# Linear attention and a gated feed-forward block: fewer dummies and another VectorE order in the first batch's start

## The chip, the cores and the metric

The kernel runs on one core of a Trainium2 chip. The metric is the device time of one execution in microseconds (us), the median over runs. Times inside a profile are us from the start of its span, which is about 1.8 us shorter than the execution.

## The reference, cut to what matters

```
phi(x) = where(x > 0, x, exp(x) - 1) + 1            # = max(x, 0) + min(exp(x), 1)
kv  = einsum('bhsd,bhse->bhde', phi(k), v)
z   = sum_s phi(k)
num = einsum('bhsd,bhde->bhse', phi(q), kv)
den = einsum('bhsd,bhd->bhs', phi(q), z) + 1e-6
x   = (num / den), heads side by side               # 4608 x 512
out = (silu(x @ w_gate) * (x @ w_val)) @ w_out      # 512 -> 1536 -> 512
```

There are 8 batches of 8 heads, 576 tokens and 64 dimensions each. Everything after the first x is a long stream of matmuls; before it TensorE has little to do, because batch 0 must come from memory, be put through phi, and be summed into kv and z.

## The kernel before

The program fixes the order of each engine's instructions. Only the start of batch 0 is touched. The helpers, with the lines by which the profile names them:

```python
WARM = (4, 3, 4, 4, 2, 1, 2, 2)

def warm(n, ...):            # L124: n dummies, 128x512 matmuls of ones that nobody reads
def q_turn(lp, pair_):       # L430: 16 matmuls that turn half lp of q into PSUM
    for l2 in range(2):
        for j in range(J - 1):
            nc.tensor.matmul(out=pair_[j // 4][...], lhsT=qr[0][:, 2 * lp + l2, ...], rhs=id16[:, :], ...)
def q_exp(lp, h, pair_):     # L120, ScalarE:  exp of a bank of turned q
def q_phi(lp, h, pair_):     # L442, VectorE:  max and min in one, completes phi(q)
def mx_k / mn_k / add_k:     # L143, L147, L159, VectorE: max(k, 0), min(exp(k), 1), their sum
def zt(...):                 # L396: z of half a batch, 9 matmuls for the max part, 9 for the min part
def zr_copy(...):            # L400, VectorE: z, spread to 64 columns
```

```python
    warm(WARM[0]); q_one(qa); q_one(qb)
    q_turn(0, qa);  q_exp(0, 0, qa);  q_exp(0, 1, qa)
    warm(WARM[1])
    q_turn(1, qb);  q_exp(1, 0, qb);  q_exp(1, 1, qb)
    warm(WARM[2])
    exp_k(0, 0);  exp_k(0, 1)
    q_phi(0, 0, qa);  q_phi(0, 1, qa)
    mx_k(0, 0)
    q_phi(1, 0, qb)
    mn_k(0, 0)
    mx_k(0, 1)
    zt(0, 0, X[1], kp, True, False)
    warm(WARM[3])
    zt(0, 0, X[1], ek, False, True)
    zr_copy(0, 0, X[1])
    warm(WARM[4])
    t_corners(0, Zr, 0, pp4[2]);  lnrd(pp4[2], 0)      # L254, then four log / exp on ScalarE
    mn_k(0, 1)
    q_phi(1, 1, qb)
    zt(0, 1, Y[0], kp, True, False)
    warm(WARM[5])
    zt(0, 1, Y[0], ek, False, True)
    add_k(0, 0)
    zr_copy(0, 1, Y[0])
    warm(WARM[6])
    kv_corner(0, 0, kp, True, True)                    # L185, the kv product
    ...                                                # then x, layer 1 (L276, from fb = 2 on L292)
```

q comes in two loads. Two of its four heads are cast to 16 bits first (one of them on ScalarE); the third and fourth head are cast on VectorE when the second load has landed.

Of the kernel before, what the change touches and what calls it, by code (L numbers as in the profile page):

```python
# [17 lines left out]
def kernel(  # L18
# [21 lines left out]
    EPS = 1e-6  # L40
    SC = 4096.0
    NB = 3
    WARM = (4, 3, 4, 4, 2, 1, 2, 2)

    sb = ctx.enter_context(tc.tile_pool(name="sb", bufs=1))
    pp = ctx.enter_context(tc.tile_pool(name="ps", bufs=1, space=bass.MemoryType.PSUM))
# [72 lines left out]
    def act(out, in_, func=AF.Copy, scale=1.0, bias=0.0):  # L119
        nc.scalar.activation(out=out, in_=in_, func=func, bias=bias, scale=scale)  # L120

    def warm(n, w=512, ps=None):
        for _ in range(n):
            nc.tensor.matmul(out=(ps or pp4[1][1])[:, 512 - w:512], lhsT=ones[:, :],  # L124
                             rhs=ones[:, 0:1].to_broadcast([P, w]), start=True, stop=True)
# [4 lines left out]
    def jl(t, b, lp):  # L130
        return t[b % 2][:, lp, :, :].rearrange("p j (l d) -> p l j d", d=D)

    def lj(t, b, lp):
        return t[b % NB][:, hs(lp), :].rearrange("p l (j d) -> p l j d", d=D)

    def exp_k(b, lp):
        act(jl(ek, b, lp), lj(kr, b, lp), AF.Exp)
# [4 lines left out]
    def mx_k(b, lp):  # L142
        nc.vector.tensor_scalar(out=jl(kp, b, lp), in0=lj(kr, b, lp), scalar1=0.0, scalar2=None, op0=ALU.max)  # L143

    def mn_k(b, lp):
        a = ek[b % 2][:, lp, :, :]
        nc.vector.tensor_scalar(out=a, in0=a, scalar1=1.0, scalar2=None, op0=ALU.min)  # L147
# [246 lines left out]
    def zt(b, lp, ps, t, first, last):  # L394
        for j in range(J):
            nc.tensor.matmul(out=ps[:, 0:2], lhsT=t[b % 2][:, lp, j, :], rhs=ob[:, 0:P:C],  # L396
                             start=(first and j == 0), stop=(last and j == J - 1))

    def zr_copy(b, lp, ps):
        nc.vector.tensor_scalar(out=Zr[b][:, lp, :, :], in0=ps[:, 0:2].unsqueeze(2).to_broadcast([P, 2, D]),  # L400
                                scalar1=1.0 / SC, scalar2=None, op0=ALU.mult)

    def lnrd(ps, i, w0=0, w1=512, early=False):
        for l2 in range(2):
            act(lnt[2 * i + l2][:, w0:w1], ps[l2][:, w0:w1], AF.Ln, bias=epsb[:, 0:1])
            if not early:
                act(rd[i][:, l2, w0:w1], lnt[2 * i + l2][:, w0:w1], AF.Exp, scale=-1.0)
        for l2 in range(2 if early else 0):
            act(rd[i][:, l2, w0:w1], lnt[2 * i + l2][:, w0:w1], AF.Exp, scale=-1.0)
# [8 lines left out]
    def t_corners(g, W, lp, ps):  # L418
        for (b, j0, j1, c0) in units(g)[1]:
            corners(ps, W[b], b, lp, j0, j1, c0)  # L420

    def q_one(pair_):
        for h in range(2):
            nc.tensor.matmul(out=pair_[h][:, :], lhsT=part[:, :], rhs=ones[:, 0:1].to_broadcast([P, 512]),
                             start=True, stop=False)

    def q_turn(lp, pair_):
        for l2 in range(2):
            for j in range(J - 1):
                nc.tensor.matmul(out=pair_[j // 4][D * l2:D * l2 + D, P * (j % 4):P * (j % 4) + P],  # L430
                                 lhsT=qr[0][:, 2 * lp + l2, D * j:D * j + D], rhs=id16[:, :],
                                 start=False, stop=(j % 4 == 3))

    def q_half(lp, h):
        return qT[0][:, lp, 4 * h:4 * h + 4, :, :].rearrange("p j h c -> p (j h c)")

    def q_exp(lp, h, pair_):
        act(q_half(lp, h), pair_[h][:, :], AF.Exp, bias=m1[:, 0:1])

    def q_phi(lp, h, pair_):  # L440
        a = q_half(lp, h)
        nc.vector.scalar_tensor_tensor(out=a, in0=pair_[h][:, :], scalar=1.0, in1=a, op0=ALU.max, op1=ALU.min)  # L442
# [4 lines left out]
    qa, qb = pp4[2], pp4[0]  # L447
# [3 lines left out]
    nc.vector.tensor_copy(out=qr[0][:, 3, :], in_=q32[:, 3, :])  # L451
    warm(WARM[0])
    q_one(qa)
# [3 lines left out]
    q_exp(0, 1, qa)  # L457
    warm(WARM[1])
    q_turn(1, qb)
    q_exp(1, 0, qb)  # L460
    q_exp(1, 1, qb)
    warm(WARM[2])
    exp_k(0, 0)
# [2 lines left out]
    q_phi(0, 1, qa)  # L466
    mx_k(0, 0)
    q_phi(1, 0, qb)
    mn_k(0, 0)
    mx_k(0, 1)  # L470
    zt(0, 0, X[1], kp, True, False)
    warm(WARM[3])
    zt(0, 0, X[1], ek, False, True)
    zr_copy(0, 0, X[1])
    warm(WARM[4])
    t_corners(0, Zr, 0, pp4[2])
    lnrd(pp4[2], 0)
    mn_k(0, 1)
    q_phi(1, 1, qb)
    zt(0, 1, Y[0], kp, True, False)  # L480
    warm(WARM[5])
    zt(0, 1, Y[0], ek, False, True)
# [279 lines left out]
```

## Time and profile before

| | |
|---|---|
| median of three runs | 315.97 us (315.6 to 316.2) |
| span of the profiled execution | 314.1 us |
| TensorE busy | 98% of the span |
| kv product of batch 0 starts | 13.07 |
| steady part of layer 1 starts (first L292) | 19.48 |

Two numbers serve as mile posts from here on: the start of the kv product (L185), and the start of layer 1's steady part (L292). How the page and the chain are read is told in the prediction.

### The profile page before, as it was taken

What the parts mean: (1) busy time and instruction counts of PE and PEld (TensorE: products, weight loads), DVE (VectorE), ACT (ScalarE), POOL (GpSimd) and SP (SyncE); (2) the same over time, 40 slices, a digit from 0 to 9 for tenths busy, and PEclk for the clock granted to TensorE, in tenths of its full rate; (3) what the DMA queues carried; (4) which work ended last, traced back from release to release, by engine and by line L of the source; (5) the groups of instructions that cost most, each with busy time, mean ns of one, the idle gap of its engine ahead of it and who ended that gap; (6) DMA issues with size and microseconds to landing.
All of it is one profiled execution on the core that took longest, in us unless ns stands there. A gap on an engine that the chain in (4) does not pass through costs nothing.

```text
span 314.1 us, 5531 instructions
## 1 busy us (share of the span) xinstructions
PE 307.5 (98%) x2186; PEld 142.7 (45%) x2186; DVE 205.5 (65%) x362; ACT 152.0 (48%) x231; POOL 48.0 (15%) x72
## 2 busy tenths in 40 slices
PE   8899999999999999999999999999999999999994
PEld 4444444444544454445444544444444444444442
DVE  4854688899789767977597849874991434133410
ACT  4865839738643745366535743475330333133311
POOL 7755334300000230023000500000000000000000
PEclk9999999999999999999999999999999999999999
DMA  8999999995612396129702990314032400140014
GB/s 216 198 198 199 206 207 232 238 206 88 140 33 41 50 180 170 38 41 163 197 20 57 134 230 0 75 35 102 0 61 59 91 1 1 37 98 0 2 33 100
DMA packets 41162, 32.80 MB, mean 104 GB/s; under 512 B 16432, under 2 KB 36144, under 8 KB 41136
## 3 DMA queue, kind: packets, MB, share of 16 engines
q0 software_dynamic: 20464, 18.29, 37.2%
q1 hardware_dynamic: 20592, 14.13, 18.6%
q8 instruction: 17, 0.28, 0.4%
q14 instruction: 9, 0.07, 0.1%
q10 hardware_dynamic: 80, 0.03, 0.0%
HBM read 37.75 MB, written 9.44 MB: 150 GB/s over the span
## 4 chain that ended last, share of the span: by engine, by line
PE 96%; DMA 1%; DVE 1%; ACT 1%; issue 0%
PE pp L292 57%; PE pp L299 30%; PE pp L276 2%; PE pp L254 2%; PE pp L185 2%; DMA q<-in_q_dram 1%; PE pp L124 1%; PE pp L430 1%; ACT qT L120 0%; ACT ek L120 0%; PE pp L371 0%; PE pp L396 0%; DVE kp L159 0%; PE pp L212 0%; DVE ek L147 0%; DVE osb L322 0%
## 5 line engine op out<-in xcount | busy, mean ns | idle before, releaser
L120 ACT ACTIVATE sil<-pp 128x512 f16<-128x512 f32 x108 | 63.4, 597 | 101.8 <-PE pp L292 100.9
L292 PE MATMUL pp<-xT,wg 128*128 128x512 f16 x416 | 106.8, 379 | 0.0
L292 PE MATMUL pp<-xT,wv 128*128 128x512 f16 x416 | 106.8, 379 | 0.0
L285 DVE SCALAR_TENSOR_TENSOR hT<-pp,sil 128x512 f16<-128x512 f32 x108 | 72.4, 682 | 49.0 <-PE pp L292 35.6
L299 PE MATMUL pp<-wo,hT 128*128 128x512 f16 (+2 forms) x444 | 97.2, 374 | 0.6 <-DVE osb L322 0.6
L299 PEld LDWEIGHTS <-hT 128*128 128x128 f16 x444 | 41.9, 98 | 49.7 <-issue 2.1
L292 PEld LDWEIGHTS <-wv 128*128 128x128 f16 x416 | 40.7, 98 | 49.1
L292 PEld LDWEIGHTS <-wg 128*128 128x128 f16 x416 | 40.7, 98 | 48.4
L322 DVE TENSOR_SCALAR osb<-pp 128x512 f32<-128x512 f32 (+1 forms) x19 | 12.9, 682 | 30.6 <-PE pp L299 26.2
L120 ACT ACTIVATE osb<-pp 128x512 f32<-128x512 f32 (+1 forms) x18 | 10.3, 573 | 34.8 <-PE pp L299 34.8
L120 ACT ACTIVATE ek<-kr 128x1152 f16<-128x1152 f16 x16 | 17.8, 1156 | 0.1
L120 ACT ACT_TABLE_LOAD x13 | 16.7, 1283 | 2.3 <-PE pp L292 2.1
L693 POOL COPY gate<-qT 128x1 f16<-128x1 f16 x4 | 1.3, 320 | 97.9 <-DVE hT L285 71.2
L229 DVE TENSOR_TENSOR qp<-qp,rden 128x1152 f16<-128x1152 f16 x12 | 16.2, 1347 | 0.0
L220 DVE TENSOR_REDUCE den<-prod 128x18 f32<-128x1152 f16 x12 | 16.1, 1344 | 0.0
L271 DVE TENSOR_SCALAR xT<-pp 128x512 f16<-128x512 f32 (+1 forms) x14 | 8.8, 667 | 7.1 <-PE pp L254 7.1
L120 ACT ACTIVATE eq<-qr 128x1152 f16<-128x1152 f16 x12 | 13.2, 1147 | 0.0
L103 POOL DMA_DIRECT2D vr<-in_v_dram x16 | 11.7, 735 | 9.3 <-PE pp L292 3.5
L103 POOL DMA_DIRECT2D kr<-in_k_dram x16 | 11.7, 735 | 7.8 <-DMA wo<-in_moe_w_out_dram 1.8
L147 DVE TENSOR_SCALAR ek<-ek 128x1152 f16<-128x1152 f16 x16 | 7.7, 483 | 7.5 <-ACT ek L120 7.5
L159 DVE TENSOR_TENSOR kp<-ek,kp 128x1152 f16<-128x1152 f16 x16 | 12.1, 758 | 0.5
L103 POOL DMA_DIRECT2D qr<-in_q_dram x14 | 10.1, 723 | 5.8 <-DMA wo<-in_moe_w_out_dram 1.8
(76 smaller groups left out, 183.6 us busy)
## 6 DMA issues: line engine op xcount, KB each, us to landing
out_dram<-osb SPq DMA_DIRECT2D x70, 128.0 KB, 3.2
kr<-in_k_dram POOLq DMA_DIRECT2D x16, 288.0 KB, 8.9
vr<-in_v_dram POOLq DMA_DIRECT2D x16, 288.0 KB, 9.8
qr<-in_q_dram POOLq DMA_DIRECT2D x14, 288.0 KB, 12.1
wo<-in_moe_w_out_dram POOLq DMA_DIRECT2D x3, 512.0 KB, 12.7
wg<-in_moe_w_gate_dram POOLq DMA_DIRECT2D x5, 256.0 KB, 9.1
wv<-in_moe_w_val_dram POOLq DMA_DIRECT2D x5, 256.0 KB, 9.7
q<-in_q_dram SPq DMA_DIRECT2D x2, 576.0 KB, 4.1
```

The source lines that it names most:

```text
L103: nc.gpsimd.dma_start(out=dst[b % NB][:, 2 * lp:2 * lp + 2, :], in_=src[b].rearrange("(l a) (c j) d -> (a c) l (j d)", a=2, j=J)[:, 2 * lp ...
L120: nc.scalar.activation(out=out, in_=in_, func=func, bias=bias, scale=scale)
L147: nc.vector.tensor_scalar(out=a, in0=a, scalar1=1.0, scalar2=None, op0=ALU.min)
L159: nc.vector.tensor_tensor(out=a, in0=ek[b % 2][:, lp, :, :], in1=a, op=ALU.add)
L185: nc.tensor.matmul(out=ps[hh][D * l2:D * l2 + D, D * lp:D * lp + D], lhsT=t[b % 2][rows, lp, j, D * l2:D * l2 + D], rhs=vr[b % NB][rows, 2 ...
L220: nc.vector.tensor_reduce(out=den[:, c, :], in_=prod[:, :, :].rearrange("p j (l d) -> p (j l) d", d=D), axis=AX.X, op=ALU.add)
L229: nc.vector.tensor_tensor(out=qv, in0=qv, in1=rden[:, c, :].unsqueeze(2).to_broadcast([P, 2 * J, D]), op=ALU.mult)
L271: nc.vector.tensor_scalar(out=dst, in0=ps[l2][:, c0:], scalar1=1.0 / SC, scalar2=None, op0=ALU.mult)
L285: nc.vector.scalar_tensor_tensor(out=hT[g % 2][:, fb, :], in0=ps[1][:, :], scalar=SC, in1=s[:, :], op0=ALU.mult, op1=ALU.mult)
L292: nc.tensor.matmul(out=ps[h][:, :], lhsT=w[:, c, P * fb:P * fb + P], rhs=xT[g % 2][:, c, :], start=(c == 0), stop=(c == 3))
L299: nc.tensor.matmul(out=l2p[(g, t)][:, n0:n1], lhsT=hT[g % 2][:, fb, P * t:P * t + P], rhs=wo[:, fb, n0:n1], start=(fb == 0), stop=(fb == F ...
L322: nc.vector.tensor_scalar(out=o[:, n0:n1], in0=ps[:, n0:n1], scalar1=1.0 / SC, scalar2=None, op0=ALU.mult)
```

## The change

The intent is to shorten the chain that leads to the first real work of TensorE. Two of three dummies between the turns of q's halves go. On VectorE q's last phi moves ahead of k's first min, into a wait, so that it no longer stands in front of the add of k, and the second half's max and min move behind the first z. One dummy more covers the longer wait ahead of z's second part.

```diff
-    WARM = (4, 3, 4, 4, 2, 1, 2, 2)
+    WARM = (4, 1, 4, 5, 2, 1, 2, 2)
...
     q_phi(1, 0, qb)
+    q_phi(1, 1, qb)
     mn_k(0, 0)
-    mx_k(0, 1)
     zt(0, 0, X[1], kp, True, False)
...
     lnrd(pp4[2], 0)
+    mx_k(0, 1)
     mn_k(0, 1)
-    q_phi(1, 1, qb)
     zt(0, 1, Y[0], kp, True, False)
```

## The prediction

> **What bounds the kernel now.** I read the page first (engines, then its chain), then the chain of waits in order of time for the first 45 us, then the timelines of TensorE (PE), VectorE (DVE) and ScalarE (ACT) for the first 34 us. Times are us from the start of the span.
>
> The page, parts 1 and 4:
>
> ```profile
> PE 307.5 (98%) x2186; PEld 142.7 (45%) x2186; DVE 205.5 (65%) x362; ACT 152.0 (48%) x231; POOL 48.0 (15%) x72
> PE 96%; DMA 1%; DVE 1%; ACT 1%; issue 0%
> ```
>
> TensorE carries nearly the whole span, so only what lets it reach its real work sooner is worth anything. The change touches the first 13 us alone. There the chain hops between engines (columns: start, length, what):
>
> ```profile
> 6.23 0.76 PE pp L124 x3
> 6.99 0.61 PE pp L430 x12
> 7.60 0.02 issue
> 7.62 1.26 ACT qT L120 x2
> 8.88 1.06 ACT ek L120
> 9.95 0.02 issue
> 9.97 0.66 DVE ek L147
> 10.62 0.05 issue
> 10.67 0.39 PE pp L396 x9
> ```
>
> L124 are the dummies (matmuls whose result nobody reads), L430 the turns of q's second half, then come q's two exponentials, k's first exponential, k's min and the second part of z. So three dummies sit on the path that sets the end. From about 19.6 on the chain is layer 1, matmul behind matmul, 80 in 17.27 us (0.216 each): whatever the start gains moves all of this earlier, unless weights are late.
>
> The VectorE timeline (start, length, then line, operation and tiles, in brackets the idle time before):
>
> ```profile
> 7.93 0.46 DVE L143 TENSOR_SCALAR kp<-kr 128x1152 f16<-128x1152 f16 x1
> 8.34 0.69 DVE L442 SCALAR_TENSOR_TENSOR qT<-pp,qT 128x512 f16<-128x512 f32 x1
> 9.97 0.64 DVE L147 TENSOR_SCALAR ek<-ek 128x1152 f16<-128x1152 f16 x1 [0.94 <-ACT ek L120]
> 10.54 0.44 DVE L143 TENSOR_SCALAR kp<-kr 128x1152 f16<-128x1152 f16 x1
> 11.10 0.29 DVE L400 TENSOR_SCALAR Zr<-pp 128x128 f16<-128x128 f32 x1
> 11.30 0.45 DVE L147 TENSOR_SCALAR ek<-ek 128x1152 f16<-128x1152 f16 x1
> 11.67 0.69 DVE L442 SCALAR_TENSOR_TENSOR qT<-pp,qT 128x512 f16<-128x512 f32 x1
> 12.27 0.75 DVE L159 TENSOR_TENSOR kp<-ek,kp 128x1152 f16<-128x1152 f16 x1
> ```
>
> It shows 0.94 us of idle before k's min (9.97), and q's last phi (11.67) later, in front of the add of k (12.27) that TensorE needs.
>
> [...] the weight loads of four 512-wide matmuls between 2.31 and 3.60 start 0.43 apart, the dummies from 6.16 to 6.61 start 0.225 apart. The removed dummies thus lie after the warm-up, in this execution. [...] the order on VectorE is the order of the program, and a phi put ahead of k's min delays it if it finishes later; the trace shows all of them in program order. [...] k's first min takes 0.64, the second 0.45, and GpSimd was preparing a transfer from 9.61 to 10.35. The 11.08 preparation did not lengthen the second one, so I don't rest much on it.
>
> **The change, part by part.**
>
> 1. *Two dummies fewer before the second turns.* The last of three starts at 6.61 and takes 0.216 of issue, to 6.83; the turn starts at 6.92. The 0.09 between is what it takes here to go from full-array matmuls to 64-column ones: the corners after the dummies at 10.92 show it too (10.92 + 2 × 0.216 = 11.35, corners at 11.45, though their own input was only ready at 11.39). With one dummy: 6.16 + 0.22 + 0.09 = 6.47. The first eight turns need the cast that ends by 6.27; at 0.051 each (sixteen from 6.92 to 7.74) they go till 6.88. The other eight need the last cast, which ends at 6.77: no wait to speak of. The exponential needs twelve turns: it now starts 0.13 after the issue of the twelfth (7.49, 7.62), so it could at 6.47 + 11 × 0.051 + 0.13 = 7.16. ScalarE is then just done with q's first half: its two started at 5.99 and 6.58, next slot 7.17. So 7.17 in place of 7.62: **0.45 gained** there, and it hands on: exponentials of q at 7.17 and 7.76, of k at 8.33, end 9.49 (1.16 long). k's data must be there; VectorE read it at 7.93.
>
> 2. *q's last phi ahead of k's min.* Its exponential ends at 7.76 + 0.68 = 8.44. VectorE: max of k 7.93, phi 8.34, the moved phi 0.61 later at 8.95, then min at 9.56. k's exponential ends at 9.49, so the phi fits into what was idle time and costs about 0.05. Min ends at 10.02 (if 0.46) to 10.20 (if 0.64), before 10.61. Gain at the second part of z: 0.41 to 0.59.
>
> 3. *One more dummy in front of that part of z.* Five from 8.86 at 0.216 end at 9.94; z's second part can start at 10.08 at the earliest. It fills idle time, cost 0. TensorE waits 0.79 there now; after it about 0.2.
>
> 4. *Second max and min of k behind the first Zr copy.* Zr had to wait for z (11.06), not for the max (ends 10.98), so taking the max away from before it gives nothing by itself today; after part 2 it keeps VectorE free: z at 10.08 to 10.26, Zr at 10.51 to 10.69 (the 0.43 of before), corners at 10.85 to 11.03, ScalarE's first logarithm at 11.30 to 11.47 in place of 11.89. Max then runs at about 10.8, min 11.17, ends 11.62, add of k 11.54 to 12.29. The price: z of the second half waits for this later max. Corners end their issue near 11.27, max ends near 11.24: level. Its second part waits for min (11.62 + 0.05) and the dummy to 11.76, is issued till 12.01, two dummies to 12.44, and 0.09 more: kv product at 12.53 in place of 13.07, with its add ready at 12.29.
>
> **Sum.** Every branch (the kv product, ScalarE's eight log/exp steps, which in 11.89 to 16.95 run nearly back to back and feed the last xT at 17.01) moves by 0.4 to 0.6. I take 0.48. Behind 13 us the change touches nothing, so the rest should move as one piece: 315.97 - 0.48 = 315.5, 0.15%.
>
> **Rivals.**
>
> - *Weights late.* GpSimd's issues wait with eight transfers outstanding (counted from the releasers in its timeline), so the issue at 18.57, released by a wv load, puts that load, the one of columns 256 to 511, at about 18.5. It is needed at 20.13, 19.65 after the change: 1.1 us of slack left. Against this rival; it would make 315.97.
> - *The move costs what the dummies give.* If q's last exponential or the phi before it comes later than I think, k's min waits for the moved phi. Without part 1 it would: exponential end 8.88, phi 8.95 to 9.64, min at 9.56 still. So even then not before 9.97: against it. Or the later max holds z of the second half so long that TensorE idles; I worked out level, and a 0.2 slip would halve the gain: 315.7.
> - *The clock.* Fewer dummies are less activity. TensorE is busy from 1.06 on and the removed work is 0.43, replaced by turns that come earlier, so I see no half-rate stretch[...]. I give it 3%.
> - *Only the start gains, layer 1 then waits for something else.* The last xT (logarithm chain) and TensorE's own order are level at 17.66; if the logarithms move less than the rest, 0.1 to 0.2 is lost: 315.7.
>
> **Range and chances.** Runs of the kernel before lie at 315.6 to 316.2, a spread of 0.6, larger than the gain. 0.3 either way from gain and noise each: 315.0 to 316.1. 2% is 6.3 us; the whole touched stretch is 19 us and its gain is bounded by the idle in it, so faster by 2% is at 0.5%, slower at 0.7%.
>
> **What would show it.** Right: in the new chain one dummy in place of three, q's second exponentials at about 7.2, k's min at about 9.55 with hardly any idle before it (now 0.94), z's second part near 10.1 to 10.3, the kv product near 12.5, layer 1's steady part starting near 19.0 in place of 19.48, and the same length after. Wrong: min released by the phi well after 9.6; TensorE idle before z of the second half; dummies that start 0.43 apart after 6.2; or the first matmuls of layer 1 waiting for a load.

The sum came to 0.48 at the start, 315.97 - 0.48 = 315.5. "The warm-up" is what the two spacings show, 0.43 before and 0.225 after. The eight outstanding transfers are read off so: GpSimd prepares eight loads from 1.35 to 7.21 without waiting for a transfer, and starts the ninth at 8.19, after 0.99 of waiting, released by a load of k.

## The result

The changed kernel took 315.41 us, median of four runs (315.29 to 315.64); the kernel before, in the same set, 316.06 (315.6 to 316.2). The ratio is 0.9983 with a 95% interval of 0.9966 to 1.0000. A ratio is the mean time of one kernel's runs over that of the other's in the same rounds, so not quite the ratio of the two medians.

The page of the changed kernel, the engines:

```profile
PE 307.5 (98%) x2185; PEld 142.9 (46%) x2185; DVE 204.8 (65%) x362; ACT 152.0 (48%) x231; POOL 48.1 (15%) x72
```

TensorE is as busy as before: the two removed dummies and the added one don't show at this scale. The chain of waits of the changed kernel, in order of time (start, length, what), over the same stretch as in the prediction:

```profile
6.09 0.32 PE pp L124
6.41 0.84 PE pp L430 x12
7.25 0.02 issue
7.27 1.27 ACT qT L120 x2
8.54 1.06 ACT ek L120
9.60 0.02 issue
9.62 0.47 DVE ek L147
10.09 0.04 issue
10.14 0.39 PE pp L396 x9
```

It is the same chain with the same links. The dummies take 0.32 of it (0.76 before), twelve turns take 0.84 (0.61 before: part of the gain is given back), k's min 0.47 (0.66 before). At the second part of z the changed kernel is 10.67 - 10.14 = 0.53 ahead. The VectorE timeline of the changed kernel (start, length, instruction, in brackets the idle time before it):

```profile
8.25 1.27 DVE L442 SCALAR_TENSOR_TENSOR qT<-pp,qT 128x512 f16<-128x512 f32 x2
9.62 0.46 DVE L147 TENSOR_SCALAR ek<-ek 128x1152 f16<-128x1152 f16 x1
10.56 0.29 DVE L400 TENSOR_SCALAR Zr<-pp 128x128 f16<-128x128 f32 x1 [0.48 <-PE pp L396]
10.77 0.45 DVE L143 TENSOR_SCALAR kp<-kr 128x1152 f16<-128x1152 f16 x1
11.13 0.45 DVE L147 TENSOR_SCALAR ek<-ek 128x1152 f16<-128x1152 f16 x1
11.50 0.75 DVE L159 TENSOR_TENSOR kp<-ek,kp 128x1152 f16<-128x1152 f16 x1
```

q's last phi (the second of the two L442) has gone into the wait for k's exponential, the min starts 0.10 after it (9.52 to 9.62; the wait was 0.94), and the add of k starts at 11.50 in place of 12.27. The two mile posts on TensorE, before and then after:

```profile
13.07 0.48 PE L185 MATMUL pp<-vr,kp 64*64 64x64 f16 x36
19.48 1.03 PE L292 MATMUL pp<-xT,wg 128*128 128x512 f16 x4
```

```profile
12.50 0.48 PE L185 MATMUL pp<-vr,kp 64*64 64x64 f16 x36
18.91 1.03 PE L292 MATMUL pp<-xT,wg 128*128 128x512 f16 x4
```

The kv product starts at 12.50 (13.07), the steady part of layer 1 at 18.91 (19.48): 0.57 gained in this pair of traces, about what was predicted. The experiments ask whether every execution gains as much.

### The profile page after: what moved, and what is told of

Read it like the earlier page. It is cut to its first block, busy times and chain, and to the rows that moved or that the text cites. A ratio compares the mean times of both kernels' runs of the same rounds, so it can differ in the third digit from the quotient of the medians.

```text
span 313.5 us, 5529 instructions
## 1 busy us (share of the span) xinstructions
PE 307.5 (98%) x2185; PEld 142.9 (46%) x2185; DVE 204.8 (65%) x362; ACT 152.0 (48%) x231; POOL 48.1 (15%) x72
## 4 chain that ended last, share of the span: by engine, by line
PE 96%; DMA 1%; ACT 1%; DVE 1%; issue 0%
PE pp L292 57%; PE pp L299 30%; PE pp L276 2%; PE pp L254 2%; PE pp L185 2%; DMA q<-in_q_dram 1%; PE pp L430 1%; PE pp L124 1%; ACT qT L120 0%; ACT ek L120 0%; PE pp L371 0%; PE pp L396 0%; DVE kp L159 0%; PE pp L212 0%; DVE osb L322 0%; DVE ek L147 0%
## 5 line engine op out<-in xcount | busy, mean ns | idle before, releaser
L292 PE MATMUL pp<-xT,wv 128*128 128x512 f16 x416 | 106.8, 379 | 0.0
L292 PE MATMUL pp<-xT,wg 128*128 128x512 f16 x416 | 106.8, 379 | 0.0
L292 PEld LDWEIGHTS <-wv 128*128 128x128 f16 x416 | 40.7, 98 | 49.1
L292 PEld LDWEIGHTS <-wg 128*128 128x128 f16 x416 | 40.7, 98 | 48.4
```

What stands on the lines that cost most here:

```text
L292: nc.tensor.matmul(out=ps[h][:, :], lhsT=w[:, c, P * fb:P * fb + P], rhs=xT[g % 2][:, c, :], start=(c == 0), stop=(c == 3))
```

## The experiments

The kernels of one set ran on one chip and shared its runs of the kernel before.

### The changed kernel again, and its parts

`after5` is the changed kernel itself. `dummies_only` and `move_only` are its two parts.

> The changed kernel again, for a closer interval and a second trace. Mine (the gain is about 0.5 us at the start and is handed on whole): ratio to before 0.9975 to 0.9990, the kv product at 12.4 to 12.7, the steady part of layer 1 starting at 18.8 to 19.2. Rival (the first result was a matter of execution-to-execution phase): ratio 0.999 to 1.001.

`dummies_only`:

```diff
-    WARM = (4, 3, 4, 4, 2, 1, 2, 2)      # kernel before, order unchanged
+    WARM = (4, 1, 4, 4, 2, 1, 2, 2)
```

> The kernel before with one dummy in place of three between the turns, order of VectorE untouched. Mine (the dummies carry the gain through ScalarE's exponentials): k's exponential ends near 9.6, min at 9.6, z second part 10.15 to 10.35, kv product at 12.5 to 12.75 against 13.07 before, span shorter than before by 0.35 to 0.55. Rival (VectorE's order carries it: the moved phi in front of the add of k): add of k and kv product still near 13.0, gain under 0.15.

`move_only`:

```diff
-    WARM = (4, 1, 4, 5, 2, 1, 2, 2)      # changed kernel, new order kept
+    WARM = (4, 3, 4, 5, 2, 1, 2, 2)
```

> The new VectorE order (and the fifth dummy ahead of z's second part) with the three dummies between the turns kept. Mine: ScalarE's exponentials as before (second pair from 7.6, k's min at 9.95), kv product at 12.85 to 13.05, gain 0 to 0.2, the 0.2 only if k's min takes 0.46 rather than 0.64. Rival (order carries it): gain 0.4 or more.

| | median us | ratio to before, 95% | kv product | layer 1 |
|---|---|---|---|---|
| before, same set, 11 runs | 315.57 (315.17 to 316.38) | | | |
| `after5` | 315.39 (315.12 to 315.77) | 0.9993 (0.9980 to 1.0006) | 12.48 | 18.89 |
| `dummies_only` | 315.45 (315.16 to 315.69) | 0.9997 (0.9984 to 1.0009) | 12.52 | 18.92 |
| `move_only` | 315.60 (315.19 to 315.85) | 0.9997 (0.9984 to 1.0011) | 12.79 | 19.20 |

By the mile posts the expectations nearly held: the dummies alone bring the kv product to 12.52, the move alone to 12.79, which is 0.06 before the range that I had given it. But the times did not follow. The ratio of `after5`, 0.9993, misses my forecast (0.9975 to 0.9990) and lies in the rival's. The kernel before ran as fast as 315.17 here, within 0.05 of the best run of the changed kernel. The traces say where to look. TensorE in the changed kernel's first trace, and then in `dummies_only`:

```profile
4.90 1.18 PE L430 MATMUL pp<-id,qr 128*64 128x128 f16 x16 [0.25 <-DVE qr L448]
6.02 0.39 PE L124 MATMUL pp<-ones 128*128 128x512 f16 x1
6.37 1.09 PE L430 MATMUL pp<-id,qr 128*64 128x128 f16 x16
```

```profile
4.83 0.89 PE L430 MATMUL pp<-id,qr 128*64 128x128 f16 x16 [0.46 <-DVE qr L448]
5.65 0.39 PE L124 MATMUL pp<-ones 128*128 128x512 f16 x1
6.36 1.07 PE L430 MATMUL pp<-id,qr 128*64 128x128 f16 x16 [0.32 <-DVE qr L450]
```

The first sixteen turns are the same instructions on the same data, and took 1.18 in one execution and 0.89 in the other. Where they took 0.89, TensorE sat idle behind its single dummy (0.32) and the second turns waited for the cast of q's third head (L450). In such an execution two more dummies would have fitted into the wait almost whole (an estimate: 2 × 0.216 = 0.43 against 0.32). This gave a second theory, P: what three dummies cost depends on how late the array comes to full rate, which differs from execution to execution.

### How much is scatter, and what one dummy costs

`before_again` and `after_again` are the two kernels unchanged. `five_dummies` and `zero_dummies` change one number of the changed kernel, `WARM[1]`, from 1 to 5 and to 0.

> The kernel before against itself: how much two sets of runs of one kernel differ, and a second trace of it. Theory P (how long the first turns of q take depends on when in them the array reaches full rate, which differs from execution to execution, and the three dummies only cost time where it comes late): ratio 0.999 to 1.001; the first sixteen turns take anything from 0.9 to 1.45 us; if they take about 0.9, the second turns wait for the cast and start at about 6.4 in spite of three dummies; if about 1.4, they start at 6.9 to 7.0. Rival (three dummies always cost 0.43): second turns 0.5 behind those of the changed kernel whatever the first took.

> A third set of runs of the changed kernel, to size its gain over executions. Mine as predicted: ratio 0.9985. Theory P: the gain is an average over executions in which the dummies cost 0 to 0.4, so 0.9988 to 0.9996, and the changed kernel's runs spread less than those of the kernel before.

> The changed kernel with five dummies in place of one between the turns. Now they end later than the casts in every execution, so each costs its 0.216. Mine: second turns start at the end of the first + 5 x 0.216 + 0.09, k's exponential 0.5 to 0.8 later than in the changed kernel, kv product near 13.1 to 13.4, ratio to before 1.0000 to 1.0015. Rival (ScalarE's chain has slack that hides dummies): ratio as the changed kernel.

> The changed kernel with no dummy between the turns. Mine: the second half of these turns waits for the last cast (ends near 6.75) anyway, so q's second exponentials stay at 7.2 to 7.3, ratio as the changed kernel, difference under 0.0005. Rival (each dummy costs): another 0.2 us, ratio 0.0007 lower.

| | median us | ratio to before, 95% | kv product | layer 1 |
|---|---|---|---|---|
| before, same set, 9 runs | 315.54 (315.07 to 316.07) | | | |
| `before_again` | 315.65 (315.49 to 315.74) | 1.0002 (0.9990 to 1.0015) | 13.20 | 19.60 |
| `after_again` | 315.70 (315.43 to 316.20) | 1.0005 (0.9992 to 1.0018) | 12.55 | 18.95 |
| `five_dummies` | 315.89 (315.39 to 316.02) | 1.0012 (0.9999 to 1.0026) | 12.76 | 19.17 |
| `zero_dummies` | 315.51 (315.40 to 315.81) | 1.0000 (0.9988 to 1.0013) | 12.67 | 19.08 |

The changed kernel missed both forecasts of its ratio (0.9985 and 0.9988 to 0.9996): here it was level with the kernel before. Nor did its runs spread less, as theory P had it: by 0.77 over five runs, against 0.25 in `before_again`. None of these intervals excludes 1, and that of a kernel against itself is 0.0025 wide, while the predicted gain is 0.0015. So the times of a set can't size this change; the mile posts can. `zero_dummies` brings nothing beyond one dummy, as expected: the second half of the turns waits for the last cast, and q's second exponentials start at 7.27. (Its kv product is later, 12.67, where its second max, at 10.77, met a preparation of GpSimd, 10.39 to 11.13, and took 0.62; see below.) `five_dummies` fell into an execution with quick first turns (0.89), its second turns started at 6.82 as expected (5.63 + 5 × 0.216 + 0.09 = 6.80), and its kv product at 12.76 came earlier than the 13.1 to 13.4 that I had written down: a miss, for I had not asked which phase.

With all traces together, theory P can be read off. "Distance" is from the start of q's first cast to the start of the second turns, which takes out when q landed. "Full rate from" is the start of the first record of the granted clock in the packed trace (`0/clock` in trace.npz). A `--windows` query shows 1.00 before it too, but only because nothing is recorded there: in `after` the first turns start 0.107 apart, and the last ones, behind 5.61, 0.056 apart.

| trace | dummies | full rate from | first 16 turns | distance |
|---|---|---|---|---|
| before | 3 | 5.96 | 1.37 | 2.58 |
| `before_again` | 3 | 5.94 | 1.34 | 2.54 |
| `move_only` | 3 | 5.27 | 1.05 | 2.25 |
| `gate_before` (below) | 3 | 4.96 | 0.89 | 2.09 |
| `after5` | 1 | 6.10 | 1.44 | 2.21 |
| `after_again` | 1 | 6.17 | 1.46 | 2.22 |
| after | 1 | 5.61 | 1.18 | 1.98 |
| `dummies_only` | 1 | 3.94 | 0.89 | 2.04 |
| `five_dummies` | 5 | 4.03 | 0.89 | 2.52 |

The later the full rate, the longer the first turns. With quick first turns, two dummies fewer gain 2.09 - 2.04 = 0.05. With slow ones the distances differ by 2.56 - 2.22 = 0.34, but there the changed kernel's first turns took some 0.1 longer. Take the first turns off the distance, and 1.20 or 1.21 is left with three dummies and 0.76 to 0.80 with one (1.15 in `dummies_only`, where the cast held TensorE): at equal first turns the gain is 0.44, which is two dummies of 0.216. That is the comparison I had wanted by design, and got by chance. So the predicted 0.43 holds where the dummies end after the cast; for every execution (the rival in the expectations) it falls.

### Trying to fix the phase

To make the first turns quick in every execution, both kernels were held back at the start: q's buffer is filled three times on VectorE before its loads may go, all loads wait for that, and TensorE runs 14 more dummies meanwhile.

```diff
-    WARM = (4, 3, ...)        # after_late_q: (4, 1, ...) -> (18, 1, ...)
+    WARM = (18, 3, ...)
+    nc.vector.memset(q32[:, 2:4, :], 0.0)
+    nc.vector.memset(q32[:, 0:2, :], 0.0)
+    nc.vector.memset(q32[:, 0:2, :], 0.0)
+    nc.gpsimd.tensor_copy(out=gate[:, :], in_=q32[:, 0, 0:1])
     ...                       # then q's loads, then all others
```

> The kernel before with q's loads (and all others) held back some 5 us by fills of q's buffer, and TensorE kept busy meanwhile by 14 more dummies, so that the array is at full rate in every execution before q's first turns. Theory P (three dummies cost time only where the array warms late): the first sixteen turns take 0.9; three dummies after them end about when q's third head is cast, so the second turns start within 0.1 of that cast's end, and this kernel and the changed kernel with the same delay differ by under 0.15 us. Rival (three dummies always cost 0.43): the second turns start 0.3 or more behind the cast, and the two differ by 0.4 or more. Both are some 5 us slower than without the delay, which means nothing.

> The changed kernel with the same delay. Theory P: first turns 0.9, then TensorE waits for the cast behind its one dummy and the second turns start at the same distance from q's first cast as with three dummies (within 0.1); from q's first cast to the kv product the two kernels differ by under 0.15 us. Rival: 0.4 or more sooner than with three.

Medians were 323.26 (322.95 to 323.34) and 324.70 (324.50 to 325.03), four runs each. The kernel with fewer dummies is 1.44 us *slower*, which neither theory had foreseen. TensorE in `before_late_q`, then in `after_late_q`:

```profile
11.20 0.82 PE L124 MATMUL pp<-ones 128*128 128x512 f16 x3
14.15 1.00 PE L432 MATMUL pp<-id,qr 128*64 128x128 f16 x16 [2.13 <-DVE qr L452]
15.09 1.04 PE L124 MATMUL pp<-ones 128*128 128x512 f16 x4
```

```profile
11.21 0.39 PE L124 MATMUL pp<-ones 128*128 128x512 f16 x1
14.30 1.49 PE L432 MATMUL pp<-id,qr 128*64 128x128 f16 x16 [2.69 <-DVE qr L452]
15.72 1.89 PE L124 MATMUL pp<-ones 128*128 128x512 f16 x4
```

The delay had an unwanted effect: q's second load now started beside k's and v's, and landed so late that its cast started at 13.64 and 13.78, 3.77 and 3.90 behind q's first cast (1.47 in the plain kernel). In both kernels the second turns followed the cast (its end at 14.10 and 14.24), so here two dummies fewer gained nothing, as theory P says for a late cast. But behind three dummies TensorE was idle for 2.13, behind one for 2.69, and in `after_late_q` the granted clock fell to 0.50 at 13.4, in this gap, and came back to 1.00 at 20.2: four dummies take 1.89 in place of 1.04, and the kv product starts at 22.29 in place of 20.50. All four runs of `after_late_q` have a mean clock of 0.989. So has one untraced run of `before_late_q` (323.34; the others 0.997 or 0.998): its clock seems to have fallen too, at a place where that cost next to nothing. So the experiment did not give the clean comparison it was made for. It showed instead what two more dummies were worth here: a low mean clock in one run of four in place of four of four.

### The long min, and a version beyond the change

k's first min took 0.64 in the trace before and 0.46 after, which makes up 0.18 of the 0.57. `gate_before` is the kernel before with GpSimd held until this min is done:

```diff
     mn_k(0, 0)
+    nc.gpsimd.tensor_copy(out=gate[:, :], in_=ek[0][:, 0, J - 1, 2 * D - 1:2 * D])
+    ...                        # load of wv 256:512 and the loads behind it, moved here
```

> The kernel before with GpSimd held by a copy that reads the result of k's first min, so that it prepares the second slice of the value weights after that min and not beside it. If GpSimd's preparation is what stretched the min (0.64 and 0.50 in two traces, 0.46 elsewhere): the min takes 0.44 to 0.47, and what may be stretched instead is the max or the second min behind it, which now meet the preparation. Rival (the min is long because ScalarE writes the same tile's other half, or by chance): it still takes 0.5 or more.

VectorE and GpSimd in `gate_before` (start, length, instruction):

```profile
9.67 0.46 DVE L147 TENSOR_SCALAR ek<-ek 128x1152 f16<-128x1152 f16 x1 [0.69 <-ACT ek L120]
10.82 0.66 DVE L147 TENSOR_SCALAR ek<-ek 128x1152 f16<-128x1152 f16 x1
```

```profile
10.19 0.35 POOL L459 COPY gate<-ek 128x1 f16<-128x1 f16 x1 [1.28 <-DVE ek L147]
10.48 0.74 POOL L460 DMA_DIRECT2D wv<-in_moe_w_val_dram  x1
```

The first min is back at 0.46, and the second, which now meets the preparation (10.48 to 11.22), takes 0.66. The stretch moved with GpSimd's preparation, as expected. In `before_again` it fell mainly on the second min (0.73), in `dummies_only` on the max (0.65). But an instruction that meets a preparation is not always the one to be stretched. GpSimd in the kernel before, then in the changed kernel:

```profile
9.61 0.74 POOL L112 DMA_DIRECT2D wv<-in_moe_w_val_dram  x1 [0.66 <-DMA kr<-in_k_dram]
```

```profile
9.47 0.91 POOL L112 DMA_DIRECT2D wv<-in_moe_w_val_dram  x1 [0.67 <-DMA kr<-in_k_dram]
```

In the changed kernel the min began 0.15 behind the start of the preparation and kept its 0.46, and the preparation took 0.91; in the kernel before it began 0.36 behind and took 0.64. So the 0.18 hangs on where the min falls. The change moves it forward by 0.35 and so can take it out of the stretch (0.45 or 0.46 in the three traces of the changed kernel, 0.64 and 0.50 in the two of the kernel before), but how often it does is not shown. This trace also had quick first turns, and is the one that the table above uses. The kernel took 315.45 at the median, ratio to before 1.0017 (0.9990 to 1.0044); of its four runs three lie within 0.02 of that and one is at 317.29 with no trace, which stays unexplained.

If the chain is ScalarE's exponentials, then k's min, it must shorten when k's exponential goes ahead of q's last one. `k_exp_early` does this, on top of the change:

```diff
-    WARM = (4, 1, 4, 5, 2, 1, 2, 2)
+    WARM = (4, 1, 4, 4, 2, 1, 1, 2)
     q_exp(1, 0, qb)
-    q_exp(1, 1, qb)
     warm(WARM[2])
     exp_k(0, 0)
+    q_exp(1, 1, qb)
     exp_k(0, 1)
     ...
     q_phi(1, 0, qb)
-    q_phi(1, 1, qb)
     mn_k(0, 0)
+    mx_k(0, 1)
     ...
-    mx_k(0, 1)
+    q_phi(1, 1, qb)
     mn_k(0, 1)
```

> The changed kernel with k's first exponential put in front of q's last one on ScalarE, k's second max ahead of and q's last phi behind the Zr copy, one dummy fewer in two places. If the path at the start is ScalarE's exponentials, then k's min (mine): min starts near 9.05 in place of 9.62, z's second part near 9.55, the kv product near 11.95 in place of 12.50, span another 0.4 to 0.6 shorter than the changed kernel. Rival (k's data or TensorE's own order is the bound already): kv product at 12.3 or later, no further gain.

> The version with k's first exponential ahead of q's last one, again on another set of runs, to see whether it beats the kernel before beyond the scatter of the sets. Mine: ratio to before 0.9965 to 0.9985, kv product at 11.9 to 12.2, its median 0.4 to 0.9 us below. Rival (the first set was lucky): ratio above 0.999.

In `k_exp_early` VectorE's first min and the add of k:

```profile
9.16 0.46 DVE L147 TENSOR_SCALAR ek<-ek 128x1152 f16<-128x1152 f16 x1
11.28 0.75 DVE L159 TENSOR_TENSOR kp<-ek,kp 128x1152 f16<-128x1152 f16 x1
```

The min came 0.46 sooner than in the changed kernel, the kv product started at 12.09 and layer 1 at 18.49, with slow first turns (1.45). The median was 314.75 (314.64 to 314.98), ratio to before 0.9973 (0.9960 to 0.9986), against 315.39 for the changed kernel in the same set. In the second set it was 314.91 (314.61 to 315.69), ratio 0.9986 (0.9973 to 1.0000). There q's second load landed late (the cast of its third head started at 6.27, not near 5.85) and k's did too (its max at 8.47), and the kv product started at 12.59. So it beats the kernel before, by a little more than the scatter in the first set and by about as much in the second; it beats the changed kernel in the first set, and in the second that kernel did not run. In the second set the kv product missed my forecast (11.9 to 12.2), the ratio by 0.0001. The version also has one dummy fewer ahead of the kv product: with both, it would start at about 11.68 + 2 × 0.216 + 0.09 = 12.20, so some 0.1 of the gain is this dummy's (an estimate from the trace; the two were not run apart). What differs between its two traces is when data landed: k's max at 8.04 and 8.47, the kv product at 12.09 and 12.59.

## Why the prediction was right, and where it was not

The time was right: 315.41 against 315.5, in the range. That it came within 0.1 is partly luck: the sets scatter by more (see the sum below).

- *What bounds it.* Right. The chain of the changed kernel has the same links, and from the kv product on it moves as one piece.
- *Part 1, the dummies.* The mechanism was right, the size only for one kind of execution. The second turns started at 6.37 (predicted 6.47), the exponential at 7.27 (7.17), gaining 0.35 in place of 0.45. "No wait to speak of" for the last cast was too generous: sixteen turns took 1.09 in place of 0.89. And the step "the removed dummies thus lie after the warm-up, in this execution" should have gone on to ask what another execution does: with quick first turns the cast takes the dummies' place, and the gain is 0.05 instead of 0.44.
- *Part 2, the phi ahead of the min.* Right: the min started at 9.62 (predicted 9.56), released by k's exponential. In `after_again`, where k landed later, the phi held it, at 9.68. One reading was incomplete: the 11.08 preparation left k's second min at 0.45, but itself took 0.98 in place of 0.74. There GpSimd's preparation was lengthened and the min was not, as with the preparation of 0.91 beside the first min of the changed kernel.
- *Part 3, the fifth dummy.* Right: TensorE still waited 0.26 there (predicted about 0.2).
- *Part 4, max and min behind Zr.* Right within 0.06 at every step, counted from the case of the quick min: Zr 10.56, corners 10.91, first logarithm 11.36, max 10.77, min 11.13, add ending at 12.25, kv product 12.50 (predicted 12.53). That the move gives "nothing by itself" was nearly so: `move_only` reached 12.79 with three dummies and middling first turns.
- *The sum.* 0.48 predicted for the start; 0.57 and, for `before_again` against `after_again`, 0.65 seen at layer 1. Over the runs less arrived: the three sets of the changed kernel differ from their own runs of the kernel before by -0.54 (4 runs), -0.22 (6) and +0.19 (5) in the mean, weighted by runs -0.17. Two causes were shown, the phase of the array's clock (0.44 against 0.05 at the second turns) and the stretched VectorE instruction (0.18 in the first trace). The stretch from the first L292 to the start of the last ScalarE instruction also differs among the five traces of the two kernels, from 290.97 to 291.40, with the same instructions. In the twelve traces the full rate came before or with the first turns in three, midway in two, and near their end or later in seven. That is too few to say how often each phase comes up, so what the change is worth on average stays open: between nothing and 0.5 us.
- *The rivals.* Weights late was not seen in any trace. "The move costs what the dummies give" was not seen. The clock did not fall in the changed kernel (mean 0.997 to 1.000 in its fifteen runs; the one fall in its first trace, at 312.81, is behind the last matmul), but `after_late_q` showed what I gave 3%: with q's second load as late as there, the clock fell to 0.50 from 13.39 to 20.22 and the kernel with fewer dummies took 1.44 us more.

## What to carry to other kernels

At the start of a kernel an instruction's duration can depend on when the array comes to full rate (the same sixteen turns took 0.89 to 1.49 here), so read the same few instructions in several traces before you size a gain of half a microsecond from one. Here dummies cost time only where the work behind them was ready (two of them 0.44, and 0.05 where a cast held it); and with late data the kernel with two fewer lost its clock and 1.44 us, so before taking one out ask how long TensorE would then stand idle if that data came late. Where two engines hand a chain back and forth, look at the order on the engine that feeds the chain: k's exponential ahead of q's last one, with one dummy fewer, moved the kv product from 12.50 to 12.09 on top of the change.

## What else the traces show

- In `after_late_q` the granted clock fell to 0.50 at 13.39, 1.79 after the last matmul, in a gap of 2.69, and came back to 1.00 at 20.22, 5.9 after TensorE was busy again. In `before_late_q` TensorE was idle for 2.13 at the same place and the next four dummies took the usual 1.04 (mean clock 0.998). What decides when the clock falls was not shown.
- In the twelve traces without a delay the first dummy always starts at 1.06, and the full rate begins between 3.94 and 6.64, 2.70 apart; the first sixteen turns took 0.89 to 1.49.
- The step from full-array dummies to 64-column turns cost 0.10 beyond the 0.216 of the last dummy (6.37 to 6.69 in `k_exp_early`). Its cause was not shown.
- In the same twelve traces the six max and min that began 0.27 to 0.51 behind the start of an unlengthened preparation (0.74 to 0.76) ended 1.00 to 1.02 behind it. The eight that began 0.08 to 0.23 behind kept 0.45 or 0.46, and the preparation took 0.84 to 0.99.
